# A forward chain dealt anew, one hand order over most of the kernel, and a backward sweep that starts ahead of its chain

## The chip, the core and the metric

The kernel runs on one core of a Trainium2 chip. The core has a matrix engine (PE, whose weight loads are shown apart as PEld), a vector engine (DVE), a scalar engine (ACT), a general engine (POOL) and a synchronising engine (SP); each runs its own instructions in order, and waits on semaphores for the others. Transfers are issued from SP, or from POOL, and run on 16 DMA engines. PE writes into PSUM, a small memory of banks; everything else lies in SBUF or in device memory. The metric is the device time of one execution in microseconds. Lower is better.

## What is computed

A gate mixes two networks over the same 2048 tokens of width 576, and the kernel returns the output and the gradients of every input.

```python
def _A_ref(x, wq, wk, wv, wo):          # 32 heads of 18, one shared key and value
    scores = einsum('bhqd,bkd->bhqk', q, k) * Dh ** (-0.5)
    o = einsum('bhqk,bkd->bhqd', softmax(scores), v)
    return o.transpose(...).reshape(B, S, H * Dh) @ wo
def _B_ref(x, mem0, Wq, Wk, Wv, Wo, seg_len):   # 32 heads of 128, segments of 32 tokens
    for s in range(n_seg):
        h = concatenate([mem, xs], axis=1)       # 8 memory tokens and 32 of the segment
        q, k, v = (einsum('btd,dhe->bhte', h, W) for W in (Wq, Wk, Wv))
        p = softmax(where(mask, einsum('bhqe,bhke->bhqk', q, k) * scale, -1e9))
        o = einsum('bhte,hed->btd', einsum('bhqk,bhke->bhqe', p, v), Wo)
        mem = o[:, :M, :]                        # goes into the next segment
g = sigmoid((x * gate_w).sum(-1)); out = g * _A_ref(...) + (1 - g) * _B_ref(...)
```

Network B is a recurrence: the memory rows of a segment must be done before the next begins, forward, and after it, backward. Network A has no such order.

## The kernel before

The kernel runs in stages: a setup with A's projections, the projections of grad_out and x through B's weights, a **forward weave**, a bulk stage for the tokens of B (`b_bulk`), a **backward weave**, the token gradients (`b_post`), the weight gradients (`b_dw`), and A's end. Each stage has its own pools of SBUF and PSUM tiles; a tile of a new pool that lies where an old one lay waits for the old one's last user.

`weave` takes two generators. The *chain* does the recurrence of B on the 8 memory tokens of each of 64 segments, cut by `yield` into 16 pieces a segment; the *sweep* does A's attention, 1024 steps of one key block against one pair of heads. A weave issues one piece and then one step, in that order on every engine; `lead` is how many steps go first (2 forward, none backward).

*A forward sweep step* (`a_pass1`): PE computes S of the next step (`a_S`, one buffer) and dP of this one, ACT the exponential `a_E` of S, DVE the product `a_W` of dP and `a_E`, in two halves, and PE adds `a_W` and `a_E` times the keys and values to `a_acc`. After 16 steps a block of 512 queries is done; `a_post` turns it, in three parts at the steps 2, 3 and 5 of the next 16: PE transposes the sums (`a_acs` into `a_tk`) and the block's QD, ACT copies the latter to `a_qt`, and POOL normalises and scales, with three stores from SP.

*A forward chain segment* (`b_chain_fwd`): projections of q, k and v for 32 rows, in units `proj(w, j, kts, name)` of up to five quartets of matmuls each (one quartet an element of kts), into the PSUM tiles `c_x` or `c_pj` (one buffer each); transposes by selection (`mem_T`); scores into c_x, their exponential c_E, the denominators `den` into a new c_x, the reciprocal `c_rd` on DVE, `c_pn`, its expansion `c_PB` on POOL; the output `po` and c_oT; and `heads(lo, hi)`, four matmuls a head through Wo, in two pieces of 16 heads. `rows_out`, `rows_copy`, `head_out` and `mT_out` store results; `load_k` and `load_v` fetch c_kx and c_vx for the next segment; `stash` and `stash_end` transpose a weight through SP into st_WT.

*Around the weaves.* At the end of `a_pass1` four small transposes go through `a_dlT`, which shares its one buffer with `a_qt`, to dl_dram. `b_bulk` builds two masks and zeroes four tiles on POOL, and loads its chunks (x_q, x_dO, x_k and others) from SP into the same pool as its results. Before the backward weave `load_WoT` loads WoT; the chain's first segment loads its inputs and then the weights WT (14.2 MB in six transfers, `load_WT`), and the backward sweep (`a_pass2`) loads a chunk of QD and SD for every four steps.

The two weaves, `b_bulk`, `b_post` and the two projection stages are issued in the order written; what lies between them (load_Wo, make_WoT, load_WoT, the last part of the setup) is ordered by a scheduler.

## Time and profile before

Three runs took 6164.37, 6149.91 and 6148.34 us, the median 6149.91 us. The profiled execution took 6158.5 us, its span is 6156.7 us.

| stage | from, to (us of the span) | length | PE busy | DMA share |
|---|---|---|---|---|
| setup, A's projections | 0, 184 | 184 | 138.59 | 0.43 |
| load of Wo, WoT | 184, 215 | 31 | 15.13 | 0.85 |
| projection of grad_out | 215, 361 | 146 | 137.54 | 0.61 |
| projections of x | 361, 500 | 139 | 130.92 | 0.41 |
| forward weave | 500, 2313 | 1813 | 1731.88 | 0.60 |
| bulk stage | 2348, 3060 | 712 | 654.01 | 0.93 |
| backward weave | 3098, 4765 | 1667 | 1515.68 | 0.42 |
| token gradients | 4775, 5345 | 570 | 548.55 | 0.96 |
| weight gradients | 5378, 6055 | 677 | 669.74 | 0.71 |
| end of A | 6055, 6157 | 102 | 87.49 | 0.27 |

Over the whole span PE is busy 92%, DVE 61%, ACT 56%, POOL 32%. A row of the timeline gives start and duration of one instruction or a run of like ones, and in brackets how long its engine had been idle before it and what ended that. A busy PE isn't always PE at its peak: the granted clock of a stretch says how fast it ran.

### The profile page before, as it was taken

The page shows a single profiled execution, that of the slowest core. Times are in us where ns is not written, and L with a number is a line of the kernel's source. Part 1 is how long each engine was busy: PE and PEld are TensorE (multiplying, and loading weights), DVE is VectorE, ACT ScalarE, POOL GpSimd, SP SyncE. Part 2 cuts the span into 40 slices and gives each one's busy share as a digit, 9 for nine tenths or more (in the row PEclk, how much of TensorE's full clock was granted, in tenths as well). Part 3 has the DMA queues.
Part 4 walks back from the last instruction along what each step waited for, and adds up shares of the span by engine and source line. Part 5 has one row for each costly group of instructions (what it writes and reads, how often), then busy time and mean ns, then how long its engine had stood idle before and what let it go on. Part 6 is the DMA issues. An engine that isn't in the chain of part 4 may idle for free.

```text
span 6156.7 us, 211396 instructions
## 1 busy us (share of the span) xinstructions
PE 5649.8 (92%) x90123; PEld 3274.8 (53%) x90334; DVE 3760.5 (61%) x7124; ACT 3435.7 (56%) x4916; POOL 1957.9 (32%) x3483
## 2 busy tenths in 40 slices
PE   7898999999999996999869999999998999899999
PEld 4543444444444445777735555555555777675444
DVE  4336778777778884666568888888888111111112
ACT  3325777777777774665557777777777222111101
POOL 3002333333333344444423333333333111112213
PEclk7999999999999998999989999999999999999999
DMA  4645666666665548999864443434343999896663
GB/s 151 224 154 115 126 125 130 122 128 126 125 127 115 108 86 231 253 255 254 248 196 109 108 108 109 109 108 108 109 108 98 242 248 246 228 278 200 216 186 112
DMA packets 1369174, 990.03 MB, mean 161 GB/s; under 512 B 931805, under 2 KB 1186790, under 8 KB 1357510
## 3 DMA queue, kind: packets, MB, share of 16 engines
q1 hardware_dynamic: 1286870, 782.63, 51.6%
q0 software_dynamic: 81360, 193.86, 9.8%
q8 instruction: 708, 11.60, 0.8%
q14 instruction: 236, 1.93, 0.1%
HBM read 550.31 MB, written 385.03 MB: 152 GB/s over the span
## 4 chain that ended last, share of the span: by engine, by line
PE 40%; ACT 11%; DMA 6%; issue 3%; SPq 1%; POOL 1%; DVE 0%; POOLq 0%; DVEq 0%; ACTq 0%
ACT b_E L1577 11%; PE w_acc L73 10%; PE b_S L73 6%; PE y_pdx L73 4%; PE r_pj L73 4%; DMA dsx_dram<-x_dS 3%; PE r_x L73 2%; PE x_tr L78 2%; PE b_acc L73 2%; PE y_pk L73 1%; PE x_po L73 1%; PE x_b L73 1%; PE x_m L73 1%; PE b_dP L73 1%; PE f_big L73 1%
## 5 line engine op out<-in xcount | busy, mean ns | idle before, releaser
L1469 DVE TENSOR_TENSOR a_W<-a_dP,a_E 128x512 bf16<-128x512 f32 x2048 | 1316.1, 685 | 357.5 <-issue 133.4
L1598 DVE TENSOR_TENSOR b_dS<-b_dP,b_E 128x512 bf16<-128x512 f32 x2048 | 1313.6, 683 | 240.8 <-issue 121.9
L1577 ACT ACTIVATE b_E<-b_S 128x1024 bf16<-128x1024 f32 x1024 | 1047.8, 1023 | 447.1 <-PE b_dP L73 322.7
L1439 ACT ACTIVATE a_E<-a_S 128x1024 bf16<-128x1024 f32 x1024 | 1049.4, 1025 | 358.0 <-PE a_dP L73 233.9
L73 PE MATMUL b_S<-b_KV,b_QD 32*128 32x512 bf16 x2048 | 400.1, 381 | 158.8 <-ACT b_E L1577 101.6
L73 PE MATMUL r_pj<-WT,r_dT 128*32 128x288 bf16 x12288 | 491.8, 287 | 0.6 <-DMA WT<-st_WT 0.6
L73 PE MATMUL w_acc<-w_d,w_h 128*128 128x512 bf16 (+1 forms) x2352 | 471.0, 379 | 2.5
L73 PE MATMUL a_S<-a_QD,l_KV 32*128 32x512 bf16 x2048 | 401.3, 384 | 39.7 <-ACT a_E L1439 17.9
L73 PE MATMUL b_acc<-b_dS,b_SD 128*32 128x512 bf16 x2048 | 418.7, 390 | 0.9 <-DVE b_dS L1598 0.7
L73 PE MATMUL a_acc<-a_W,l_WK 128*32 128x512 bf16 x4096 | 413.1, 391 | 1.8 <-issue 1.2
L73 PE MATMUL a_acc<-a_E,l_VK 128*32 128x512 bf16 x4096 | 403.8, 383 | 1.8 <-issue 1.8
L73 PE MATMUL b_acc<-b_E,b_SD 128*32 128x512 bf16 x2048 | 403.2, 390 | 0.0
L73 PE MATMUL a_dP<-a_QD,l_KV 32*128 32x512 bf16 x2048 | 399.6, 387 | 0.5 <-issue 0.5
L73 PE MATMUL b_dP<-b_KV,b_QD 32*128 32x512 bf16 x2048 | 398.3, 385 | 0.0
L1063 DVE COPY y_T<-y_pt 128x512 bf16<-128x512 bf16 x256 | 97.1, 420 | 460.2 <-PE y_pt L78 460.2
L73 PEld LDWEIGHTS <-r_dT 128*32 128x32 bf16 x12288 | 332.5, 97 | 79.3 <-issue 1.3
L73 PEld LDWEIGHTS <-w_h 128*128 128x128 bf16 (+1 forms) x2688 | 229.9, 100 | 258.3 <-issue 6.6
L73 PEld LDWEIGHTS <-b_QD 32*128 32x128 bf16 x4096 | 165.0, 91 | 348.5 <-issue 284.3
L73 PEld LDWEIGHTS <-hm 128*32 128x32 bf16 x7680 | 196.8, 96 | 226.0 <-issue 49.9
L73 PEld LDWEIGHTS <-l_KV 32*128 32x128 bf16 x4096 | 129.2, 91 | 300.6 <-issue 264.1
L1049 ACT CAST y_tdk<-y_pk 128x512 bf16<-128x512 f32 x128 | 75.0, 586 | 376.7 <-PE y_pk L73 211.7
L73 PE MATMUL y_pdx<-WT,y_T 128*128 128x288 bf16 x2048 | 273.0, 287 | 0.0
(422 smaller groups left out, 11232.7 us busy)
## 6 DMA issues: line engine op xcount, KB each, us to landing
b_QD<-qd_dram SPq DMA_DIRECT2D x256, 128.0 KB
b_SD<-sd_dram SPq DMA_DIRECT2D x256, 128.0 KB
dOx_dram<-p_tok SPq DMA_DIRECT2D x16, 1024.0 KB
c_vx<-vx_dram SPq DMA_DIRECT2D x256, 64.0 KB
krow_dram<-c_k POOLq DMA_DIRECT2D x64, 256.0 KB
qrow_dram<-c_q POOLq DMA_DIRECT2D x64, 256.0 KB
vrow_dram<-c_v POOLq DMA_DIRECT2D x64, 256.0 KB
x_q<-qx_dram SPq DMA_DIRECT2D x32, 512.0 KB
```

The lines of the kernel that those rows point to most:

```text
L73: return self.nc.tensor.matmul(out, lhsT, rhs, start=start, stop=stop, tile_position=tp, skip_group_check=True)
L78: return self.nc.tensor.transpose(out, in_, self.identB[b:b + nrows, b:b + nrows], tile_position=tp)
L1049: nc.scalar.copy(d[w][:, r, :], pk[:])
L1063: nc.vector.tensor_copy(T_[t][w][:], pt[:])
L1439: nc.scalar.activation(E_[n][:], S.pop(n)[:], ACT.Exp, scale=SCALEA)
L1469: nc.vector.tensor_tensor(out=W_[n][:, i, :], in0=dP[i][:], in1=E_[n][:, i, :], op=ALU.mult)
L1577: nc.scalar.activation(E_[n][:], S.pop(n)[:], ACT.Exp, scale=SCALEA)
L1598: nc.vector.tensor_tensor(out=D_[n][:, i, :], in0=dP[i][:], in1=E_[n][:, i, :], op=ALU.mult)
```

## The change

- *Forward chain.* Still 16 pieces a segment, filled differently: the k and q projections start with single quartets and swap c_x and c_pj; the mask is added with four 64-column matmuls; scores, den and the low half of v's second unit (`vlo`, 256 columns) share one c_x tile `px`; the high half goes to c_pj and is copied by DVE; the heads are in three pieces of 11, 10 and 11; `load_v` stands before `head_out`.
- *a_post.* QD is no longer transposed on PE and copied on ACT; SP fetches it with a transposing transfer from qd_dram. The f32 transposes are split, one at step 1 and three at step 2. The last block's three stores go through POOL's queue.
- *One hand order* from load_Wo to b_post, with no scheduler between the stages.
- *Bulk stage.* The masks are built in `setup_B_consts`, the four tiles are zeroed on DVE, and the loads have a pool `xl`.
- *Backward weave.* The sweep leads by 12 steps, and does 10 more after the chain's pieces 5 and 8; WoT is loaded inside `b_chain_bwd`; WT comes in halves of its columns (rows of 576 bytes) instead of halves of its heads.

```diff
@@ setup_B_consts
+        mb = pool.tile([P, 64], BF16, name="mbias")
+        nc.gpsimd.memset(mb[:], NEGB)
...
+        mx = pool.tile([P, 4, P], BF16, name="maskX")
+        mxm = pool.tile([P, 4, 32], BF16, name="maskM")
+        nc.gpsimd.memset(mx[:], 0.0)
+        nc.gpsimd.memset(mxm[:], NEGB)
+        for j in range(4):
+            nc.gpsimd.affine_select(out=mx[:, j, :], in_=mx[:, j, :], compare_op=ALU.is_ge, fill=NEGB,
+                                    base=0, pattern=[[-1, P]], channel_multiplier=1)
...
+        self.maskX, self.maskM = mx, mxm
@@ weave, proj_cols
-    def weave(self, chain, sweep, per_piece, lead=0):
-        with self.tc.manual_schedule():
-            for _ in range(lead):
-                next(sweep)
-            for _ in chain:
-                for _ in range(per_piece):
-                    next(sweep, None)
-            for _ in sweep:
-                pass
+    def weave(self, chain, sweep, lead, extra=()):
+        for _ in range(lead):
+            next(sweep)
+        extra = dict(extra)
+        for i, _ in enumerate(chain):
+            for _ in range(1 + extra.get(i, 0)):
+                next(sweep, None)
+        for _ in sweep:
+            pass
...
+                        start=(kt == 0), stop=(kt == NKT - 1), tp=(0, 32 * c))
+
+    def proj_cols(self, out, st, Wt, lo, n, kts):
+        for kt in kts:
+            for c in range(4):
+                self.mm(out[32 * c:32 * c + 32, :], lhsT=st[:, kt, :], rhs=Wt[:, kt, c * 1024 + lo:c * 1024 + lo + n],
                         start=(kt == 0), stop=(kt == NKT - 1), tp=(0, 32 * c))
 
@@ b_chain_fwd
             yield
-            proj("k", 0, (0, 1, 2), "c_x")
-            yield
-            proj("k", 0, (3, 4), "c_x")
-            proj("k", 1, (0,), "c_pj")
-            yield
-            proj("k", 1, (1, 2, 3), "c_pj")
-            yield
-            proj("k", 1, (4,), "c_pj")
-            proj("q", 0, (0, 1), "c_x")
-            yield
-            proj("q", 0, (2, 3, 4), "c_x")
-            yield
+            proj("k", 0, (0,), "c_pj")
+            yield
+            proj("k", 0, (1, 2, 3), "c_pj")
+            yield
+            proj("k", 0, (4,), "c_pj")
+            proj("k", 1, (0, 1, 2), "c_x")
+            yield
+            proj("k", 1, (3, 4), "c_x")
+            proj("q", 0, (0,), "c_pj")
+            yield
+            mT_out("k", self.mem_T(t2["k"], psum, "c_x", 1))
             rows_out("k")
-            proj("q", 1, (0, 1, 2), "c_pj")
+            proj("q", 0, (1, 2), "c_pj")
+            yield
+            proj("q", 0, (3, 4), "c_pj")
+            proj("q", 1, (0,), "c_x")
             if s < 48:
                 wt = stash(2 * s)
             yield
-            proj("q", 1, (3, 4), "c_pj")
-            mT_out("k", self.mem_T(t2["k"], psum, "c_x", 1))
+            proj("q", 1, (1, 2, 3, 4), "c_x")
+            rows_copy("k")
             yield
             src = self.mem_T(t2["q"], psum, "c_x", 1)
             qT = sp.tile([P, 8, 4, 8], BF16, name="c_qT", bufs=1)
...
-            rows_copy("k")
-            ps = psum.tile([P, P], F32, name="c_x", bufs=1)
-            self.mm(ps[:], lhsT=self.identB[:], rhs=self.mbias[:], start=True, stop=False)
+            px = psum.tile([P, 512], F32, name="c_x", bufs=1)
+            ps, den = px[:, 0:P], px[:, P:192]
+            for c in range(4):
+                self.mm(px[32 * c:32 * c + 32, 64:128], lhsT=self.identB[:, 32 * c:32 * c + 32],
+                        rhs=self.mbias[:], start=True, stop=False, tp=(0, 32 * c))
...
+            nc.scalar.activation(Et[:].rearrange("p a b -> p (a b)"), ps, ACT.Exp, scale=SCALEB)
+            proj("v", 0, (2, 3), "c_pj")
+            yield
+            proj("v", 0, (4,), "c_pj")
+            self.mm(den, lhsT=self.blockones[:], rhs=Et[:, 0, :], start=True, stop=False)
+            self.mm(den, lhsT=self.blockones[:], rhs=Et[:, 1, :], start=False, stop=True)
             rd = sp.tile([P, 64], F32, name="c_rd", bufs=1)
-            nc.vector.reciprocal(rd[:], den[:])
-            if not last:
-                kx = load_k(s + 1)
-            yield
-            proj("v", 1, (0, 1, 2), "c_x")
+            nc.vector.reciprocal(rd[:], den)
             pn = sp.tile([P, 2, 64], BF16, name="c_pn", bufs=1)
             nc.vector.tensor_tensor(out=pn[:], in0=Et[:], in1=rd[:].unsqueeze(1).to_broadcast([P, 2, 64]), op=ALU.mult)
             PB = sp.tile([P, 16, 4, 8], BF16, name="c_PB", bufs=1)
             self.expand(PB[:], pn[:].rearrange("p a (u q) -> p (a u) q", q=8), 16)
             nc.gpsimd.dma_start(self.pm_dram[s], pn[:].rearrange("p a b -> p (a b)"))
-            yield
+            if not last:
+                kx = load_k(s + 1)
+            vlo = px[:, 256:512]
+            self.proj_cols(vlo, h_, self.W["v"], 512, 256, (0, 1, 2))
+            yield
+            self.proj_cols(vlo, h_, self.W["v"], 512, 256, (3, 4))
+            nc.scalar.copy(t2["v"][:, 4:6, :].rearrange("p u e -> p (u e)"), vlo)
+            pv = psum.tile([P, 512], F32, name="c_pj", bufs=1)
+            self.proj_cols(pv[:, 0:256], h_, self.W["v"], 768, 256, range(NKT))
+            nc.vector.tensor_copy(t2["v"][:, 6:8, :].rearrange("p u e -> p (u e)"), pv[:, 0:256])
             rows_copy("q")
-            proj("v", 1, (3, 4), "c_x")
-            yield
+            yield
+            mT_out("v", self.mem_T(t2["v"], psum, "c_x", 1))
             po = psum.tile([P, 8, 32], F32, name="c_pj", bufs=1)
             for u in range(8):
                 self.mm(po[:, u, :], lhsT=vx[:, u, :], rhs=PB[:, u].rearrange("p c q -> p (c q)"), start=True, stop=False)
...
-            mT_out("v", self.mem_T(t2["v"], psum, "c_x", 1))
...
-            head_out()
...
-                heads(0, 16)
+                heads(0, 11)
+            yield
+            head_out()
+            if not last:
+                heads(11, 21)
             yield
             rows_copy("v")
             if not last:
-                heads(16, 32)
+                heads(21, 32)
                 hs = sp.tile([P, P], BF16, name="c_hs", bufs=1)
                 nc.vector.tensor_copy(hs[:], ph[:, 0:P])
@@ b_bulk
 
-    def b_bulk(self, wp, sp, psum):
+    def b_bulk(self, wp, lp, sp, psum):
         nc = self.nc
...
-            nc.gpsimd.memset(t[:], 0.0)
+        for t in mB["v"] + mB["k"]:
+            nc.vector.memset(t[:], 0.0)
         mT = {}
         C = {}
...
+                            mT[tt][x] = lp.tile([P, 4, HB, 8], BF16, name=f"x_{x}mT", bufs=2)
@@ load_WT, b_chain_bwd
     def load_WT(self):
-        for wi in (2, 0, 1):
-            for g in range(2):
-                self.nc.sync.dma_start(self.WT[wi][:, 16 * g:16 * g + 16, :], self.st_WT[wi][:, 16 * g:16 * g + 16, :])
+        for hf in range(2):
+            c = slice(288 * hf, 288 * hf + 288)
+            for wi in (2, 0, 1):
+                self.nc.sync.dma_start(self.WT[wi][:, :, c], self.st_WT[wi][:, :, c])
 
     def b_chain_bwd(self, keep, sp, psum):
         nc = self.nc
         NSEG = self.NSEG
         dm = [keep.tile([P, NKT, 32], BF16, name=f"dm{i}") for i in range(2)]
+        self.load_WoT(keep)
         mrow = {w: keep.tile([P, 8, n * E], BF16, name=f"r_{w}") for w, n in (("q", 1), ("k", 1), ("dx", 2))}
         pads = {w: keep.tile([P, n, 8, 32], BF16, name=f"r_{w}pad") for w, n in (("p", 1), ("ds", 1), ("x", 2))}
         for t in dm + list(mrow.values()) + list(pads.values()):
@@ a_pass1
                     bb = n // 16 - 1
-                    post = self.a_post(bb // 4, bb % 4, acs, QD.pop(bb), sp, xps, dl_all)
+                    QD.pop(bb)
+                    post = self.a_post(bb // 4, bb % 4, acs, sp, xps, dl_all)
             if n < NP_ and n % 16:
                 acc_mm(acc, n, E_, self.VK, False, False)
-            if post is not None and n % 16 in (2, 3, 5):
+            if post is not None and n % 16 in (1, 2, 5):
                 if next(post, "end") == "end":
                     post = None
             yield
...
             nc.scalar.copy(dlT[:], ptr[:].rearrange("p a b -> p (a b)"))
             nc.gpsimd.dma_start(self.dl_dram[:, t4 * 512:(t4 + 1) * 512], dlT[:])
@@ a_post
-        nc = self.nc
-        pt = psum.tile([P, 4, P], F32, name="c_pj", bufs=1)
+    def a_post(self, p, qb, acs, sp, psum, dl_all):
+        nc = self.nc
+        dq_ = nc.gpsimd if (p, qb) == (NPR - 1, self.T // 512 - 1) else nc.sync
+        qt = sp.tile([P, 4, 4, 32], BF16, name="a_qt", bufs=1)
+        nc.sync.dma_start_transpose(qt[:].rearrange("p a b c -> p a (b c)"), self.qd_dram[p][:, qb * 512:(qb + 1) * 512])
+        pt = psum.tile([P, 4, P], F32, name="c_x", bufs=1)
         for j in range(4):
             nc.tensor.transpose(pt[:, j, :], acs[:, j * P:(j + 1) * P], self.identF[:])
+            if j == 0:
+                yield
         tk = sp.tile([P, 4, 2, 64], F32, name="a_tk", bufs=1)
         tkf = tk[:].rearrange("p a b c -> p (a b c)")
         ptf = pt[:].rearrange("p a b -> p (a b)")
         nc.scalar.copy(tkf, ptf)
-        yield
-        pd = psum.tile([P, 4, P], BF16, name="c_pj", bufs=1)
-        for j in range(4):
-            self.tr(pd[:, j, :], QD[:, j * P:(j + 1) * P], P)
-        qt = sp.tile([P, 4, 4, 32], BF16, name="a_qt", bufs=1)
-        nc.scalar.copy(qt[:].rearrange("p a b c -> p (a b c)"), pd[:].rearrange("p a b -> p (a b)"))
         yield
         rl = sp.tile([P, 4, 2, 2], F32, name="a_rl", bufs=2)
         nc.vector.reciprocal(rl[:, :, 1, :], tk[:, :, :, 18])
...
-        nc.sync.dma_start(otd(self.otok_dram), ot[:].rearrange("p a b c -> p a (b c)"))
+        dq_.dma_start(otd(self.otok_dram), ot[:].rearrange("p a b c -> p a (b c)"))
@@ build_full
+        with ExitStack() as man:
+            man.enter_context(tc.manual_schedule())
+                k.load_Wo(bwo)
...
-                    k.weave(k.b_chain_fwd(a2k, cfs, cfp), k.a_pass1(a2k, a2s, a2p, cfp), 1, 2)
+                        k.weave(k.b_chain_fwd(a2k, cfs, cfp), k.a_pass1(a2k, a2s, a2p, cfp), 2)
+            with SB("xw") as xw, SB("xl") as xl, SB("xs") as xs, PS("xp") as xp:
+                k.b_bulk(xw, xl, xs, xp)
-                k.load_WoT(rk)
-                    k.weave(k.b_chain_bwd(rk, rs, rp), k.a_pass2(a3k, a3s, a3p), 1)
+                    k.weave(k.b_chain_bwd(rk, rs, rp), k.a_pass2(a3k, a3s, a3p), 12, ((5, 10), (8, 10)))
```

## The prediction

> **What bounds the kernel now.** I read first the windows, to see which stages leave PE idle; then the groups and the waits of the two weaves; then the timeline, step by step. In the windows the columns are length, busy time (and instructions) of PE, PEld, DVE, ACT and POOL, granted clock, DMA share, GB/s.
>
> ```profile
> 500.00:2313.00 1813.00, 1731.88 (x35522) 769.70 (x35523) 1439.85 (x2622) 1389.70 (x1792) 694.72 (x1438) 0.99 0.60 119
> 2313.00:2348.00 35.00, 2.34 (x16) 1.58 (x15) 0.00 (x0) 2.31 (x4) 15.56 (x25) 0.50 0.46 132
> ...
> 3060.00:3098.00 38.00, 8.46 (x90) 4.71 (x87) 4.66 (x8) 3.29 (x7) 7.72 (x13) 0.61 0.83 257
> ...
> 3098.00:3112.00 14.00, 11.27 (x230) 5.12 (x228) 9.36 (x18) 9.77 (x13) 3.78 (x6) 0.83 1.01 427
> 3112.00:3133.00 21.00, 0.39 (x16) 0.28 (x12) 0.50 (x1) 0.55 (x2) 1.20 (x3) 0.60 1.06 412
> ```
>
> The forward weave (1813 us) is PE-bound on average; three holes stand out: 35 us before the bulk stage, some 30 us before the backward weave, and 21 us inside it in which only the DMA engines work, at 412 GB/s.
>
> Inside the forward weave one segment is 16 sweep steps, each with one chain piece behind it. A step's floor is S, exp, S again, because a_S has one buffer: the a_S starts 1409.53 and 1411.08 below are 1.55 us apart.
>
> ```profile
> L1469 DVE TENSOR_TENSOR a_W<-a_dP,a_E 128x512 bf16<-128x512 f32 x2048 | 1316.1, 685 | 357.5 <-issue 133.4
> L1439 ACT ACTIVATE a_E<-a_S 128x1024 bf16<-128x1024 f32 x1024 | 1049.4, 1025 | 358.0 <-PE a_dP L73 233.9
> ...
> L1512 ACT COPY a_qt<-c_pj 128x512 bf16<-128x512 bf16 x64 | 37.1, 580 | 0.7 <-PE c_pj L78 0.6
> ```
>
> The timeline around one softmax (start, duration; PE, then DVE, then PE's heads piece):
>
> ```profile
> 1407.84 0.39 PE L73 MATMUL a_S<-a_QD,l_KV 32*128 32x512 bf16 x2
> 1409.37 0.23 PE L73 MATMUL c_x<-c_E,blockones 128*128 128x64 bf16 x2
> 1409.53 0.39 PE L73 MATMUL a_S<-a_QD,l_KV 32*128 32x512 bf16 x2
> 1410.30 0.82 PE L73 MATMUL c_x<-Wv,hm 128*32 128x512 bf16 x12
> 1411.08 0.39 PE L73 MATMUL a_S<-a_QD,l_KV 32*128 32x512 bf16 x2
> ...
> 1408.36 1.29 DVE L1469 TENSOR_TENSOR a_W<-a_dP,a_E 128x512 bf16<-128x512 f32 x2 [0.33 <-ACT c_E L401]
> 1409.63 0.56 DVE L408 RECIPROCAL c_rd<-c_x 128x64 f32<-128x64 f32 x1
> ...
> 1415.83 0.91 PE L73 MATMUL c_pj<-WoN,c_oT 128*8 128x144 bf16 x42 [0.32 <-issue]
> ```
>
> The reader is to see that the sweep's own PE work takes 0.77 us (1409.53 to 1410.30), that the reciprocal c_rd waits on DVE for the step's two a_W and ends 2.35 us after that step's S (1407.84 to 1410.19), and that c_x is written again only at 1410.30.
>
> **Forward re-deal.** From each a_E to the next, averaged over the 64 segments, the 16 steps sum to 28.21 us: 24.80 of floor (16 x 1.55) and 3.41 over it. Of these the two heads steps are 0.97 (2.07 and 2.00), the two with a_post's transposes 1.67 (2.39 each), the rest 0.77.
> After: three heads pieces of 40 to 44 matmuls, 0.77 + 44 x 0.0174 (two such lines, 64 matmuls, fill 1.11) = 1.54, under the floor; but the idle on issue (0.32 above, 0.48 in the next piece) goes with the number of instructions, so I keep 0.70. The QD transposes (0.33 of PE) and the 0.22 wait for a_qt (0.58 on ACT) go; the f32 transposes (0.15 each) come 1 and 3. With 0.24 + 0.07 for a projection quartet, memT 0.3, scores 0.6, the other pieces stand over the floor by: n=2 0.07, n=4 0.25, n=6 0.11, n=8 0.27, n=9 0.15, n=10 0.55, n=12 0.12, three more 0.08. Sum 1.60.
> The piece of n=11 is the new wait. It puts den, c_rd's source, and the low columns of v into one tile px, so the first vlo matmul must wait for c_rd, in the same piece; before, a whole step lay between them. PE is at S + 0.77 + 0.31 (v0 quartet) + 0.16 (den) = S + 1.24; c_rd ends at S + 2.35, the matmul starts near 2.40 and the next S stands behind twelve 256-column matmuls (0.42): step 2.82, 1.27 over the floor, of which 1.17 is the wait. Everything behind it on PE, the next S first, waits too. Sum 1.60 + 1.27 + 0.70 = 3.57 against 3.41: +0.16 x 64 = **+10 us**. Bounds: without the wait 10 - 75 = -65; with nothing of the issue stalls hidden and the 0.42 us DVE copy of vhi (nearest row c_qT, 0.42) in the way of a_W, +60.
> The Trainium skill, "PSUM — Partial Sum Buffer", Terms, says that two engines must not touch one bank in the same quadrant at once; by that rule the wait would be there even with separate tiles in that bank, and it speaks against putting den and vlo together. Before, den's c_x is likewise rewritten (1410.30) only after c_rd has read it (1410.19).
> SP gets 64 more DMA transposes; the like c_wt ones take 1.19 us of SP. SP's waits in the weave include 217.6 us for POOL c_oh, and head_out now stands behind the c_vx loads, so I let the two cancel and price a late SP in a rival. POOL's a_qt multiply then waits for a landing instead of ACT; POOL is busy 695 of 1813 us, which covers it.
>
> **The two holes between stages.**
>
> ```profile
> 2331.78 0.58 ACT L1493 COPY a_dlT<-c_x 64x512 bf16<-64x512 bf16 x1 [20.02 <-DMA sd_dram<-a_qt]
> ...
> 2343.66 0.33 SPq L577 DMA_DIRECT2D x_q<-qx_dram  x1
> ...
> 3072.73 10.81 SPq L839 DMA_TRANSPOSE r_vxT<-vx_dram  x1
> ...
> 3093.57 4.84 SPq L820 DMA_DIRECT2D WT<-st_WT  x6
> 3098.49 0.40 SPq L1556 DMA_DIRECT2D b_QD<-qd_dram  x1
> ...
> 3133.05 0.61 PE L73 MATMUL b_S<-b_KV,b_QD 32*128 32x512 bf16 x2 [20.66 <-DMA b_QD<-qd_dram]
> q1 hardware_dynamic: 1286870, 782.63, 51.6%
> ```
>
> *Before the bulk stage.* POOL builds masks and memsets from 2305.4 to 2320.9 between a_post's last operations, a_dlT waits 20 us for a store of the tile it shares, and x_q is issued only at 2343.66, PE starting at 2347.25. After, the loads have their own pool and stand right behind the last chain DMAs; a_dlT has two buffers of another tag; the last stores go to POOL's queue (three, 0.55 each). The POOL chain from a_rl to a_qt needs some 6 us without the memsets, four dl stores 0.55 each and about 2 to land, and the first x_qT copy waits for these: about 2323 instead of 2347, **-24 us** (-12 if the four stores stay serial over 12 us; -32 if the loads alone decide, the stage being DMA-bound).
>
> *Before and in the backward weave.* The sweep's loads now come first on SP behind the store at 3067.06 (3.5 us), so the first b_S starts near 3075.5 instead of 3097.5. But SP is in order. QD and SD of the fourth and fifth chunk wait for steps 4 and 9 to free buffers, so WoT is issued near 3092.5; then r_vmT 0.7, r_vxT 10.8, and the run from r_pT to r_q 7.5 (3083.59 to 3091.13): WT at about 3113 instead of 3093.6. The sixth chunk's QD is issued behind all six WT loads. In the rows above a QD issued just behind WT (3098.49) was there only at 3133.05: the queue is first in, first out, so it took 35 us. The lead of 12 and six interleaved steps use 18 of the 20 steps loaded, the ten extra ones stop after two, and PE with its hand order stands still until that QD lands.
> How long WT takes is unknown: its rows shrink from 18,432 to 576 B, 24,576 packets. Lower bound 14.2 MB at 412 GB/s, 34 us. Upper: the queue's mean packet is 608 B and took 39.5 ns (51.6% of 16 x 6156.7 us over 1,286,870), so 24,576 x 39.5 / 16 = 61 us. I take 47, between: QD lands at 3161 (3147 to 3175).
> By the Trainium skill, "DMA: Bandwidth & Descriptors", Specifications, rows of 512 B and more still run at line rate; that would be the 34 us, and a sum 13 us lower.
> From 3161: 18 lone steps x 1.55 = 28, then 986 pairs x 1.606 ((4765 - 3133) / 1016), then 32 chain pieces without a sweep, two segments. One costs at least its own PE work, 11.5 us (1515.7 / 64 - 16 x 0.76), at most its 26 in the weave; I take 17.5 for the evacuations between: 35. End 3161 + 28 + 1583 + 35 = 4807 against 4765: **+42 us** (+16 with 3147 and 23; +73 with 3175 and 52).
>
> **Start.** POOL builds the masks in the setup, ahead of the a_wo loads (9.48) and xtail that PE waits for (12.11, 33.51): the same operations took 2305.4 to 2311.1, 5.7 us; **+5** (0 to 8). The four p_x loads stand on SP behind the st_WoT stores (204.69, 10.43 long), so the first projection starts near 218 instead of 214.59: **+3** (0 to 5).
>
> **Sum.** +10 - 24 + 42 + 5 + 3 = +36. The profiled execution took 6158.5 us (span 6156.7), 8.6 over the median of the runs shown, 6149.91; I put the sum on the median: 6186.
>
> **Rivals.**
> *A, faster: the reciprocal isn't in vlo's way.* If DVE is ahead at that place, so that c_rd runs as soon as den is there (S + 1.24), 1.17 x 64 = 75 us go: 6111. For it: a_W's row has 357 us idle, and the 0.33 ahead of the a_W at 1408.36 need not recur. Against: DVE works in order, both a_W are issued first and need that step's dP. It decides from a wait under 0.6 us.
> *B: the early sweep does what it is for.* The QD of chunk six lands without WT's backlog; then no 21 us hole, S 22 us earlier, 35 of tail and 4 of WoT waiting: -5 instead of +42: 6139. Against it: the 20.66 row.
> *C, slower still: SP falls behind.* 64 transposes of 1.19 and a POOL that waits for their landing push PB and the k and v loads late by 1 us a segment: +64, 6250. For it: SP already waits 201.8 us on st_WT. Against: 0.60 DMA share, and SP's issue time is short of the 28 us.
>
> **How the numbers follow.** Main case 0.52, own range 6150 to 6222 (the backward bounds and half the forward ones), nearly all slower: 0.46 slower, 0.05 same, 0.01 faster. A 0.17, all faster. B 0.18: 0.09 faster, 0.07 same, 0.02 slower. C 0.13 slower. About 0.3% (18 us) is what a measurement can tell from no change. Faster 0.27, same 0.12, slower 0.61. The range runs from A to just short of C: 6108 to 6245.
>
> **What would show it.** Right: PE c_x<-Wv 32x256 idle on DVE c_rd, 1.1 to 1.2 us, 64 times; PE idle some 40 us on DMA b_QD after the twentieth b_S; two bare segments at the end of the backward weave; x_tr near 2323; no L1512 copy. Wrong: that wait absent, or b_QD landing before WT.

## The result and the profile after

The changed kernel took 6243.35 us (median of four runs, 6236.93 to 6248.59) against 6157.14 for the kernel before on the same chip: a ratio of 1.0138, with an interval of 1.0115 to 1.0161. It is 86 us slower where 36 were forecast. Its profiled execution has a span of 6234.9 us, 78.2 over that of before. Told by the first and last PE instruction of each stage's tiles:

| from, to | before | after | difference | forecast |
|---|---|---|---|---|
| start to the first p_pb | 214.6 | 222.0 | +7.4 | +8 |
| first p_pb to the first a_S | 286.1 | 289.8 | +3.7 | 0 |
| forward weave, first to last a_S | 1804.1 | 1856.5 | **+52.4** | +10 |
| last a_S to the first x_tr | 42.5 | 22.1 | -20.4 | -24 |
| bulk stage | 718.9 | 717.0 | -1.9 | 0 |
| last x_po to the first b_S | 31.3 | 8.3 | -23.0 | } |
| first to last b_S | 1663.5 | 1693.1 | +29.6 | } +42 |
| last b_S to token gradients | 12.1 | 49.4 | +37.3 | } |
| token gradients | 604.8 | 594.6 | -10.2 | 0 |
| weight gradients, end of A | 778.7 | 782.1 | +3.4 | 0 |

The three backward rows make +43.9. The -10.2 of the token gradients is no gain to count on: in the experiments below, kernels with the same code there took 594 to 608 us.

The windows of the changed kernel, in the columns of the prediction's:

```profile
515.00:2368.00 1853.00, 1708.18 (x36689) 781.48 (x36689) 1465.46 (x2680) 1337.94 (x1723) 690.98 (x1402) 0.99 0.63 121
2368.00:2392.00 24.00, 7.41 (x70) 4.01 (x67) 7.18 (x11) 5.03 (x9) 10.37 (x22) 0.63 0.74 187
...
3160.00:3195.00 35.00, 0.00 (x0) 0.00 (x0) 0.00 (x0) 0.00 (x0) 0.00 (x0) 0.50 1.12 323
4809.00:4847.00 38.00, 31.08 (x760) 21.83 (x756) 7.30 (x20) 8.29 (x19) 17.33 (x30) 0.87 0.23 58
```

Between the first and the last a_S PE is busy 17 us less than before (1709.7 against 1726.9) in 52 us more time, so it isn't the amount of work that grew. The last two rows are the stop behind WT, in which no engine does anything, and the bare tail, in which PE has 760 matmuls in 38 us.

The backward part of the timeline has the forecast's queue in its order:

```profile
3131.23 0.33 SPq L1576 DMA_DIRECT2D b_QD<-qd_dram  x1
...
3133.87 1.47 SPq L555 DMA_DIRECT2D WoT<-st_WoT  x3
...
3147.86 37.30 SPq L840 DMA_DIRECT2D WT<-st_WT  x6
...
3192.87 0.38 SPq L1576 DMA_DIRECT2D b_QD<-qd_dram  x1
...
3196.34 0.61 PE L75 MATMUL b_S<-b_KV,b_QD 32*128 32x512 bf16 x2 [40.15 <-DMA b_QD<-qd_dram]
```

WoT is held until 3133.87 by the buffers that the lone steps must free, the first WT is issued at 3147.86, and the b_S that needs the next QD starts at 3196.34 after 40.15 us of idle.

The waits of the forward weave of the changed kernel (waiting engine and line, what it waited for, us in total, times, longest):

```profile
POOL a_qt L1559 <- DMA a_qt<-qd_dram: 226.0, 51, 10.4
...
ACT a_E L1459 <- issue: 102.1, 72, 4.6
...
PE c_x L75 <- DVE c_rd L432: 65.4, 64, 2.2
...
PE c_pj L75 <- issue: 26.5, 23, 4.1
...
PE c_pj L75 <- POOL c_PB L236: 8.5, 9, 1.9
```

The wait on c_rd is there 64 times, 1.02 us each. So the forecast's new wait came nearly as it was priced (1.17), and the 42 us that were not forecast are elsewhere. To find them, take each of the 16 steps of a segment (from one a_E to the next) by its median over the 64 segments, and what its mean is over that, its excess: the median shows the deal of the work, the excess what happens in some segments only.

| us a segment | before | after | difference x 64 |
|---|---|---|---|
| medians of 16 steps | 27.28 | 27.41 | +8 |
| excess, first six steps (the heads in three of them, a_post) | 0.88 | 0.97 | +6 |
| excess, last four steps (scores, softmax, po) | 0.02 | 0.62 | **+38** |
| other | 0.03 | 0.03 | 0 |

The median of the step with the c_rd wait is 2.77 us (2.82 forecast), and the medians in all give +8 (with the wait). The rest is irregular: 38 of 52 us are in the last four steps, which had no irregular loss before; PE's idle on issue there (it waits for nothing that the profile shows), in gaps over 0.4 us, went from nothing to 12 us. By what PE does, the 40 us of excess that these steps have are 13 of idle on issue, 8.5 of waiting for c_PB and 16 of PE being busy longer than in the median; over all steps the 104 us of excess (59 before) are 41 of idle on issue (28) and 34 of longer busy time (17). Four rows of the timeline of one segment (start, duration, engine; in brackets the idle time before) show an irregular stop in a heads piece, five more how SP comes to be late:

```profile
1283.38 0.39 PE L75 MATMUL a_S<-a_QD,l_KV 32*128 32x512 bf16 x2
...
1288.81 0.52 PE L75 MATMUL c_pj<-WoN,c_oT 128*8 128x144 bf16 x9 [4.15 <-issue]
...
1289.27 0.60 PE L75 MATMUL a_S<-a_QD,l_KV 32*128 32x512 bf16 x2
...
1289.96 1.02 ACT L1459 ACTIVATE a_E<-a_S 128x1024 bf16<-128x1024 f32 x1 [4.61 <-issue]
...
1298.32 1.22 SPq L1523 DMA_TRANSPOSE a_qt<-qd_dram  x1
...
1304.76 1.05 POOL L1559 TENSOR_TENSOR a_qt<-a_qt,a_rl 128x512 bf16<-128x512 bf16 x1 [1.20 <-DMA a_qt<-qd_dram]
...
1305.83 0.33 SPq L1562 DMA_DIRECT2D sd_dram<-a_qt  x1
...
1306.26 1.20 SPq L314 DMA_TRANSPOSE c_wt<-in_B_Wk_dram  x1
...
1307.31 0.40 PE L75 MATMUL c_x<-c_qT,c_kx 128*32 128x8 bf16 x32
```

At 1288.81 PE resumes in the midst of a heads piece, 35 of whose 44 matmuls ran before, after 4.15 us in which no wait had held it. (ACT's row ends in issue too, but its exponential starts 0.09 us after the end of the a_S that it reads, so it waited for PE.) Behind the stop an a_S takes 0.60 us, ahead of it 0.39: the granted clock is 0.50 from 1288.6 on, for 6.8 us. That is part of the longer busy time. Past the weave's first steps the clock stands at 0.50 eight times for 3.4 or 6.8 us, 34 us in all (before three times, 14 us), each time after PE had been idle for some 1.5 us or more of the 6.8 ahead. At 1298.32 SP issues the new transposing transfer a_qt; POOL multiplies its result, SP must store that (1305.83), and only then comes the next transposing transfer, c_wt, beside the scores piece (1307.31). SP is in order, so each transfer runs where SP has come to, not where the program has it: in the first 51 of the 64 blocks SP issues a_qt three to eight steps after PE has made the transposes beside which it is written, in the last 13 none to two.

The trace has a control in itself: weights are moved (c_wt, st_WT) in the segments 0 to 47 alone. In the segments 1 to 48 the excess is 1.83 us a segment, in 50 to 63 it is 0.45 (before: 1.00 and 0.11), and 33 of PE's 35 stops over 0.4 us lie before segment 50.

### The profile page after: what moved, and what is told of

Its sections match the earlier page's. It is cut to its first block, busy times and chain, and to the rows that moved or that the text cites. A ratio compares the mean times of both kernels' runs of the same rounds, so it can differ in the third digit from the quotient of the medians.

```text
span 6234.9 us, 214080 instructions
## 1 busy us (share of the span) xinstructions
PE 5645.8 (91%) x91339; PEld 3294.1 (53%) x91550; DVE 3794.9 (61%) x7192; ACT 3389.5 (54%) x4852; POOL 1955.4 (31%) x3481
## 4 chain that ended last, share of the span: by engine, by line
PE 34%; ACT 11%; issue 9%; DMA 5%; SPq 2%; POOL 2%; DVE 0%; POOLq 0%; DVEq 0%; ACTq 0%
ACT b_E L1597 10%; PE w_acc L75 10%; PE b_S L75 6%; PE r_pj L75 4%; PE r_x L75 3%; DMA dsx_dram<-x_dS 3%; PE x_tr L80 2%; PE b_acc L75 2%; PE x_po L75 1%; PE x_b L75 1%; PE x_m L75 1%; PE f_big L75 1%; PE b_dP L75 1%; PE x_S L75 1%; SPq L840 1%
## 5 line engine op out<-in xcount | busy, mean ns | idle before, releaser
L75 PEld LDWEIGHTS <-hm 128*32 128x32 bf16 x8960 | 226.6, 97 | 238.1 <-issue 79.6
```

Of the source, the lines that this page charges most:

```text
L75: return self.nc.tensor.matmul(out, lhsT, rhs, start=start, stop=stop, tile_position=tp, skip_group_check=True)
```

## The experiments

The runs are in five sets, each on a chip of its own, and the irregular stops differ by chip: the changed kernel itself had a ratio of 1.0225 on another. So kernels are compared with those of the same set and by ratio to the kernel before. The forward weave of the changed kernel runs unchanged in e3, e7 and e9, which are the controls of sets 1, 2 and 3. Sets 4 and 5 have none, and of before there is one trace, not one a chip. The table has for each run the forward weave by segment (its mean, the medians, the excess at the heads, first six steps, and at the softmax, last four); PE's idle on issue in gaps over 0.4 us at the same two places, us in the whole weave; and the backward weave from the last x_po to the token gradients.

| run | median us | ratio (interval) | mean | medians | excess | issue | backward |
|---|---|---|---|---|---|---|---|
| before |  | 1 | 28.21 | 27.28 | 0.88, 0.02 | 24, 0 | 1707 |
| after | 6243.35 | 1.0138 (1.0115 to 1.0161) | 29.03 | 27.41 | 0.97, 0.62 | 27, 12 | 1751 |
| *set 1* | | | | | | | |
| e1_qt_plain | 6222.41 | 1.0114 (1.0099 to 1.0129) | 28.67 | 27.42 | 0.54, 0.68 | 9, 1 | 1752 |
| e2_den_last | 6232.95 | 1.0130 (1.0115 to 1.0146) | 28.94 | 26.79 | 0.95, 1.17 | 10, 29 | 1750 |
| e3_lead0 | 6204.18 | 1.0084 (1.0068 to 1.0099) | 28.90 | 27.42 | 0.65, 0.80 | 15, 14 | 1716 |
| e4_quiet | 6171.20 | 1.0030 (1.0017 to 1.0044) | 27.92 | 27.38 | 0.16, 0.35 | 1, 0 | 1750 |
| *set 2* | | | | | | | |
| e5_before_quiet | 6326.48 | 1.0214 (1.0199 to 1.0229) | 30.80 | 28.48 | 0.34, 1.93 | 4, 0 | 1706 |
| e6_quiet_den | 6257.79 | 1.0101 (1.0084 to 1.0118) | 29.12 | 26.62 | 0.59, 1.84 | 2, 17 | 1751 |
| e7_lead6_spread | 6303.11 | 1.0180 (1.0163 to 1.0197) | 30.36 | 27.92 | 0.99, 1.42 | 20, 31 | 1711 |
| e8_all | 6213.47 | 1.0031 (1.0019 to 1.0043) | 28.99 | 26.59 | 0.47, 1.84 | 1, 13 | 1716 |
| *set 3* | | | | | | | |
| e9_after_again | 6316.77 | 1.0225 (1.0200 to 1.0249) | 30.09 | 27.68 | 0.90, 1.44 | 15, 28 | 1752 |
| e10_wt_quiet | 6230.84 | 1.0090 (1.0072 to 1.0109) | 28.53 | 27.41 | 0.45, 0.62 | 6, 10 | 1747 |
| e11_qt_early | 6299.06 | 1.0201 (1.0178 to 1.0225) | 29.70 | 26.87 | 1.28, 1.46 | 45, 59 | 1752 |
| e12_best | 6230.41 | 1.0094 (1.0073 to 1.0115) | 29.53 | 26.86 | 1.22, 1.37 | 38, 51 | 1706 |
| *set 4* | | | | | | | |
| e13_before_wt_quiet | 6243.16 | 1.0101 (1.0073 to 1.0128) | 29.46 | 27.31 | 1.99, 0.11 | 28, 0 | 1708 |
| e14_old_deal | 6214.92 | 1.0048 (1.0032 to 1.0063) | 29.49 | 27.29 | 2.00, 0.11 | 21, 0 | 1703 |
| e15_qt_quiet | 6333.51 | 1.0248 (1.0218 to 1.0277) | 30.37 | 27.41 | 1.01, 1.87 | 41, 9 | 1750 |
| e16_all_quiet | 6263.90 | 1.0135 (1.0107 to 1.0163) | 30.09 | 26.62 | 1.57, 1.84 | 56, 8 | 1704 |
| *set 5* | | | | | | | |
| **e17_stages_only** | **6161.17** | **0.9963 (0.9949 to 0.9978)** | 28.66 | 27.48 | 1.02, 0.04 | 13, 0 | 1704 |
| e18_quiet_stages | 6206.56 | 1.0038 (1.0023 to 1.0053) | 29.07 | 27.42 | 0.17, 1.37 | 1, 0 | 1705 |

The theories that an expectation numbers are those of its own set.

### Which transfer makes the stops: e1 and e4

e1 fetches QD by a plain transfer instead of a transposing one, at the same place (so QD lies untransposed in a_qt, and what is stored from it is not the scaled QD):

```diff
-        nc.sync.dma_start_transpose(qt[:].rearrange(...), self.qd_dram[p][:, ...])
+        nc.sync.dma_start(qt[:].rearrange(...), self.qd_dram[p][:, ...])
```

> The changed kernel with one edit: a_post's transfer of QD is a plain one of the same 128 KB, without the transpose (so sd_dram holds untransposed rows and what is computed from it differs). The forward weave's steps were 29.03 us a segment against 28.21 before; their medians explain 0.13 of that, the rest is idle of PE on issue, 1.62 us a segment over the medians against 0.93. Theory 1, the 64 new transposes (512 packets of 256 B each) delay the fetch of instructions: the excess falls back to about 0.95, the run is 40 to 45 us faster than the changed kernel, near 6200. Theory 2, the excess comes from the new deal itself (where its own loads and its dense pieces now lie): it stays at 1.4 to 1.6, the run within 12 us of the changed kernel, near 6240.

e4 leaves a_qt as it is and moves the others: c_kx and both c_wt of a segment are written among the projections, in its first pieces:

```diff
             if s:
+                kx = load_k(s)
...
             proj("k", 0, (1, 2, 3), "c_pj")
+            if s < 48:
+                wt = stash(2 * s)
...
-            if not last:
-                kx = load_k(s + 1)
...
-                if s < 48:
-                    stash_end(*wt)
-                    wt = stash(2 * s + 1)
```

> The changed kernel with the forward chain's own transposing transfers (c_kx and the two c_wt of a segment) issued in the pieces 0 to 5, where PE has 40 to 56 instructions a step, instead of beside the scores and the heads, where it has 90 to 180; a_post's stay. Theory 1, PE idles on issue where such transfers run beside dense pieces: the excess over the medians falls from 1.62 to under 0.9 us a segment, the run is 40 to 60 us faster, near 6190. Theory 2, the idle goes with the density of instructions alone: the excess stays above 1.4, the run within 15 us of 6243.

Against the control on the same chip, e3 with 28.90 us a segment, e1 takes 0.23 a segment (15 us) and e4 0.98 (63 us), with the medians unmoved (27.42, 27.42, 27.38): all of it is excess, 1.48 in the control, 1.25 and 0.54. e4 stands below the weave of before (27.92 against 28.21, though on another chip). The waits of e4:

```profile
PE c_x L75 <- DVE c_rd L436: 63.7, 64, 1.1
...
POOL a_qt L1558 <- DMA a_qt<-qd_dram: 41.2, 15, 3.9
PE c_x L75 <- DMA c_kx<-kx_dram: 13.6, 10, 2.5
...
PE c_pj L75 <- issue: 1.1, 3, 0.7
```

PE's idle on issue is all but gone (29 us in gaps over 0.4 us in the control, 1 here), POOL's wait for a_qt is 41 us where the control had 271, and the c_rd wait is unmoved. What is left irregular is mainly a c_kx that now lands late in ten segments. So most of the excess hangs on where the chain's transposing transfers stand in SP's order, with the same deal of the work. By which way isn't separated: e4 lowers PE's idle on issue, POOL's wait and PE's longer busy time (35 us in the control, 12) at once, while e1, which takes 20 us of the idle on issue away, leaves POOL's wait long (319 us).

### Is the c_rd wait worth taking away: e2, e6

Both write three quartets of vlo ahead of den, so that c_rd has nothing to hold up; e6 also has e4's order, with c_kx in the last piece.

```diff
-            self.mm(den, lhsT=self.blockones[:], rhs=Et[:, 0, :], start=True, stop=False)
+            vlo = px[:, 256:512]
+            self.proj_cols(vlo, h_, self.W["v"], 512, 256, (0, 1, 2))
+            self.mm(den, lhsT=self.blockones[:], rhs=Et[:, 0, :], start=False, stop=False)
```

> The changed kernel, with the first three quartets of vlo issued ahead of den in the same piece, so that no matmul of that piece waits for c_rd (PE idled 65.4 us on it in 64 places). Theory 1, that wait is on the path that sets the step: the step falls from 2.77 to about 1.7 us, the run is 55 to 70 us faster than the changed kernel, near 6180. Theory 2, what is waited for there is waited for again a piece later (vlo's last quartets, c_PB or a_W): less than 25 us come back, near 6225.

> The changed kernel with the quiet transfers (c_kx now issued at the head of the last piece, since it came up to 2.5 us late from piece 0) and with vlo ahead of den. Theory 1, taking the c_rd wait away bought only 6 us because PE then ran into the fetch of instructions (excess 1.62 to 2.14) and into c_PB: with the fetch out of the way the median gain shows, 27.2 to 27.4 us a segment, 30 to 45 us under the quiet run, near 6135. Theory 2, c_PB and a_W are the next bound whatever the fetch does: within 12 us of the quiet run, 6160 to 6180.

In e2 the wait is gone, and its step has a median of 1.58 instead of 2.77. Yet the weave takes 28.94 us a segment where the control e3 takes 28.90. The waits of e2:

```profile
POOL a_qt L1559 <- DMA a_qt<-qd_dram: 336.2, 51, 9.2
...
PE c_pj L75 <- POOL c_PB L236: 23.5, 29, 2.0
...
PE c_x L75 <- issue: 9.3, 11, 2.0
```

POOL stands longer before a_qt (336 us, 271 in the control), its c_PB comes later (23.5 us of waiting, 14.3 in the control), and PE, which used to arrive 1 us later, now waits for it; the step two further on has a median of 2.10 instead of 1.56. In all the medians fall by 0.63 a segment (40 us), and the excess rises by 0.66 (42 us): the wait on c_rd had covered late work of POOL and late instructions. Against its control e7, e6 gains 1.24 a segment, all of it in the medians (27.92 to 26.62); its excess is as high (2.50 against 2.44). As e6 has e4's order too, its gain isn't that of e2's edit alone.

### The order on SP: e5, e9 to e11, e13 to e16, e18

e5 is the kernel before with e4's move, line for line; e13 has the lines for c_wt alone.

> The kernel before, with the same move of c_kx and the two c_wt transfers into the pieces 0 to 5. Theory 1, transposing transfers beside dense pieces cost PE fetch time whatever the deal: the excess over the medians falls from 0.93 to 0.2 to 0.4 us a segment, the run is 30 to 50 us faster than the kernel before, near 6110; then the new deal as such is worth nothing, 27.4 us of medians against 27.3. Theory 2, only the new deal suffers from them: the run is within 10 us of 6150.

> The kernel before with the two c_wt transfers of a segment moved into the pieces 2 to 5, c_kx at its place. Theory 1, transposing transfers beside the heads keep PE's instructions waiting in either deal: PE's excess falls from about 0.9 to 0.2 to 0.4 us a segment and the run is 25 to 45 us faster than the kernel before. Then the new deal had nothing of its own to give, 27.4 us of medians against 27.3. Theory 2, the old deal pays nothing for them (its stalls are the density of the two heads pieces): within 10 us of the kernel before.

Both are slower than before. In e5 the idle on issue falls to 4 us as in e4, but c_kx is late instead (144.8 us in 39 waits of up to 6.9); in e13 c_vx is:

```profile
PE c_pj L73 <- DMA c_vx<-vx_dram: 48.0, 26, 3.6
PE c_pj L73 <- issue: 23.5, 18, 2.7
```

e9 is the changed kernel; e10 is e4 without its two edits for load_k; e11 adds e2's edit and writes a_qt at the 14th step of its own block, beside the heads of the segment, instead of the first step of the next.

```diff
+                if kt == 13:
+                    b = n // 16
+                    qts[b] = sp.tile([P, 4, 4, 32], BF16, name="a_qt", bufs=1)
+                    nc.sync.dma_start_transpose(qts[b][:].rearrange(...), self.qd_dram[...])
```

> The changed kernel once more, beside the runs of this call: its stalls differ from chip to chip (in the run with lead 6 on another chip the untouched forward weave took 30.36 us a segment, not 29.03). Both theories expect medians of 27.4 us a segment and an excess of 1.6 to 3; it is the measure for the three others.

> The changed kernel with the two c_wt transfers of a segment moved into the pieces 2 to 5 and c_kx left at its place. Theory 1, PE's fetch of instructions is late where transposing transfers run beside the heads, so moving these two is enough: PE's idle on issue falls to a few us in all, the excess by at least 0.8 us a segment, the run 45 to 75 us under the changed kernel of this call. Theory 2, it was c_kx's transfer (it stood beside the scores): the excess falls by less than 0.3, the run is within 20 us.

> As the run before, and vlo ahead of den, and a_post's transposing transfer of QD issued at step 13 of its own block instead of step 1 of the next (POOL waited 226 us in all for it in the changed kernel, and with vlo first PE waited for c_PB behind it). Theory 1, the gain of taking the c_rd wait away was given back to c_PB, which is late because POOL waits for that transfer: now POOL waits under 60 us for a_qt, PE under 10 us for c_PB, 26.8 to 27.2 us a segment, 40 to 60 us under the run before. Theory 2, c_PB is late for another reason (c_pn, or the stores POOL issues): PE still waits over 25 us for it, the gain is under 25 us.

The move of c_wt alone takes 86 us from the changed kernel on that chip (6316.77 to 6230.84), half of the excess at the heads and more than half at the softmax. e11 gives nearly all of it back. Its waits:

```profile
POOL a_qt L1562 <- DMA a_qt<-qd_dram: 28.7, 16, 3.8
...
PE c_pj L75 <- issue: 62.8, 42, 5.5
...
PE c_x L75 <- issue: 20.0, 19, 4.0
```

POOL no longer waits for a_qt and c_PB is in time, so the chain of e2 is cut where it should be; but the idle on issue is six times that of e10 (104 us against 16), at the heads and the softmax alike. So a third transposing transfer among the pieces with the most matmuls seems to bring back what e10 had taken away: in the segments 50 to 63, where no weight is moved, the heads still have an excess of 1.28 us in e11 and 0.21 in e10. It isn't shown by itself, as e11 has two edits over e10; e2 alone, on another chip, had 39 us of idle on issue, and 0.63 us at those heads.

e15 is e10 with a_qt at the seventh step of its own block (`kt == 6` in e11's lines); e16 adds e2's edit and the stages of e17. e18 is e4 with those stages.

> The changed kernel with the quiet c_wt, and a_post's transposing transfer of QD issued at step 6 of its own block (at step 13 it raised PE's idle on issue, at step 1 it was late for POOL). Theory 1, what counts is only whether it runs beside a dense piece: the excess falls to 0.3 to 0.6 us a segment, 30 to 50 us under what the quiet c_wt alone gave (a ratio of 1.009 to the kernel before), a ratio of 1.001 to 1.004. Theory 2, SP blocks on the tile's one buffer and everything behind it is late: a ratio of 1.009 or more.

> As the run before, with vlo ahead of den, lead 6 and WT by halves of its heads, masks and p_x early. If the fetch of instructions was what took the c_rd gain back, the forward weave now takes 26.8 to 27.3 us a segment and the run is 60 to 100 us under the kernel before. If den's order itself brings the idle back, the excess is over 1 us a segment again and the run no better than the kernel before.

> The changed kernel with the transposing transfers of c_kx and c_wt in the pieces 0 to 5, as in the quiet run, and the same stages as the run before. If the quiet order's 27.9 us a segment holds on this chip: 35 to 50 us under the kernel before, a ratio of 0.992 to 0.994. If SP's order is too tight for c_kx, as it was in the kernel before with the same move, the ratio is 0.998 or more.

In e15 SP itself stops: a_qt has one buffer, so the transposing transfer waits for the store of the last block. In e18 the issue stalls are gone as in e4 (1.5 us), and c_kx takes their place. The queue's waits of e15 on SP, then PE's of e18:

```profile
SPq L1482 <- DMA sd_dram<-a_qt: 264.1, 63, 7.3
```

```profile
PE c_x L75 <- DMA c_kx<-kx_dram: 51.1, 28, 3.8
...
PE c_pj L75 <- issue: 1.5, 3, 0.7
```

e16 gains 0.28 a segment on e15 by e2's edit: 0.79 in the medians, of which 0.5 come back as excess. None of the orders tried brought either deal below the time of before: e5, e13, e15 and e18 each made another transfer late, and e11 brought PE's stops back.

### The backward weave: e3, e7, e8, e12, e14

e3 has no lead and no extra steps; e7 leads by six and issues one WT transfer a piece.

```diff
-                    k.weave(..., 12, ((5, 10), (8, 10)))
+                    k.weave(..., 0, ())
```

```diff
-                if s == NSEG - 1 and k == 1:
-                    self.load_WT()
+                if s == NSEG - 1:
+                    self.load_WT(k)
...
-                    k.weave(..., 12, ((5, 10), (8, 10)))
+                    k.weave(..., 6, ())
```

> The changed kernel with no lead and no extra steps in the backward weave, all else as changed (WT still in rows of 576 B). In the changed kernel the first b_S came 23 us earlier than before, PE then stood still 41 us for a QD queued behind WT, and two segments ran without a sweep for 37.7 us. Theory 1, the early start buys a longer stop and a bare tail: without it the stop is that of WT alone, some 25 to 35 us, the tail is gone, the run is 20 to 45 us faster than the changed kernel, near 6205. Theory 2, the small rows of WT are the whole loss and the lead a gain: the run is as slow as the changed one or slower, 6243 to 6265.

> The changed kernel with a lead of 6 and no extra steps, and the six WT transfers issued one by one in the first pieces instead of all at once, so that a QD has at most a part of WT ahead of it. Theory 1, the loss is the order in the queue (SP blocked on buffers, then QD behind all of WT) and the bare tail: the stop falls from 41 to under 15 us in all, the tail to about 7, the first b_S stays some 23 us early, the run is 50 to 75 us faster than the changed kernel, near 6180. Theory 2, WT's bytes must pass before the chain can go on, whatever the order: the stops still add to 30 us or more, the run is no faster than with lead 0, 6200 or more.

e3 takes 35 us off the backward weave (1716 against 1751): all of the bare tail, while the first b_S is 21 us later and the stop 8 us shorter. e7 has no long stop, yet six steps of 6 to 12 us in place of it, and ends at 1711. Before has 1707. The next three join parts: e8 is e6 with e7's backward weave, the masks built in the projection stage and the p_x loads ahead of the st_WoT stores; e12 is e11 with the same, and WT in halves of its heads (18,432-byte rows) instead of columns; e14 is e12 with the forward chain, a_pass1 and a_post of before, and c_wt moved as in e13. The lines of e12 for the start and for WT:

```diff
+                    for m in range(3):
+                        k.proj_load(items, m, pds)
                     with PS("wop") as wop:
                         k.make_WoT(bwt, wop)
...
+                        k.make_masks()
...
-    def load_WT(self):
...
+    def load_WT(self, i):
+        wi, g = (2, 0, 1)[i // 2], i % 2
+        self.nc.sync.dma_start(self.WT[wi][:, 16 * g:16 * g + 16, :], self.st_WT[wi][:, 16 * g:16 * g + 16, :])
```

> Quiet transfers, vlo ahead of den, lead 6 with WT spread, and two edits at the start: the masks are built by POOL in the projection stage where it is idle, and the first three p_x loads stand ahead of the st_WoT stores (PE waited 6.63 us for them). If the parts are independent the gains add up: about 105 in the forward weave, 60 in the backward, 7 at the start, near 6065, below the kernel before. If a part's cover is lost when another goes, the run is above 6100.

> All of it: quiet c_wt, vlo first, the early transfer of QD, masks built in the projection stage, p_x loaded ahead of the st_WoT stores, lead 6, and WT in six transfers by halves of its heads (rows of 18,432 B, as before the change), one a piece. If WT's small rows are the rest of the backward loss (45.6 us of stops with rows of 576 B however ordered, 24 before), the stops fall under 25 us; the run is 150 to 190 us under the changed kernel of this call and 50 to 90 under the kernel before. If not, the backward weave keeps over 40 us of stops and the run stays within 40 us of the kernel before.

> The forward chain, a_post and a_pass1 of the kernel before (with the quiet c_wt), and of the change the one hand order, the bulk stage's own pool and masks; the backward weave with lead 6 and WT by halves of its heads, one a piece; masks built in the projection stage and p_x ahead of the st_WoT stores. If the stages are independent: 25 to 45 us from the transfers, 20 from the gap ahead of the bulk stage, 0 to 5 from the rest, together 45 to 70 us under the kernel before. If the gap's gain depends on the new a_post, under 35.

The backward weave takes 1716, 1706 and 1703 us, so the long rows are worth some 5 to 12. A lead of six, a lead of none, one WT transfer a piece or six at once: within 13 us it is the same, and 4 us at best below before. The time of WT's 14.2 MB is paid in each, in one stop or in many: what the first 60 steps take over 1.6 us adds up to 36 to 50 us in these runs, 54 in the changed kernel and 26 before. The start is 8 us shorter with the two edits (213.7 in e8 against 222.0).

### The version that beats both: e17

The parts that stood each test are put on the forward weave of before, with its SP order untouched: the one hand order, the bulk pool, a_dlT's own buffers, the last stores on POOL, the masks in the projection stage, p_x early, a lead of six with WT one transfer a piece in halves of its heads. It is e14 without the move of c_wt.

> The kernel before with its forward chain, a_pass1 and SP order untouched (but a_dlT's tag and POOL's queue for the last block's stores), and around it the one hand order, the bulk stage's own pool, masks built in the projection stage, p_x ahead of the st_WoT stores, the backward weave with lead 6 and WT by halves of its heads, one a piece. If the stages' gains stand by themselves: 20 us from the gap ahead of the bulk stage and 0 to 5 from the backward weave, 18 to 28 us under the kernel before, a ratio of 0.995 to 0.997. If the forward weave is touched by them, over 0.998.

It takes 6161.17 us against 6183.43 on that chip, 0.9963 with an interval of 0.9949 to 0.9978: 22 us. Against the profile of before, the gap ahead of the bulk stage gives 21 (21.5 us against 42.5) and the backward weave 3. Its windows from the bulk stage's end:

```profile
3076.00:3084.00 8.00, 0.14 (x3) 0.00 (x0) 0.00 (x0) 0.59 (x1) 3.73 (x7) 0.60 0.67 203
3084.00:3130.00 46.00, 24.08 (x313) 8.32 (x314) 21.00 (x34) 17.71 (x21) 9.01 (x16) 0.65 1.01 356
```

PE is busy 24 of the 46 us in which the weights pass, at a DMA share of 1.01; before, it was busy 8.46 + 11.27 + 0.39 of 73 from 3060 to 3133.

## Why the prediction was right or wrong

*The failed step* is the one that says "the idle on issue (0.32 above, 0.48 in the next piece) goes with the number of instructions, so I keep 0.70". It made a constant, tied to the heads pieces, of what depends on when the transposing transfers run. For the three heads pieces themselves it was right: they stand over the floor by 0.67. But the sum has no other irregular loss. Of the 3.57 us a segment that it has over the floor, 2.87 are regular (1.60 and 1.27) and 0.70 irregular; measured are 4.23, of which 2.61 are in the medians, 17 us better in the whole weave, and 1.62 are excess, 59 us worse: 0.66 at the heads, 0.32 in the three steps behind them and 0.62 in the last four. These last four are what is new, with 0.02 before, and they have 38 of the 52 us by which the weave grew. e4 and e10 take more than half of the excess away without touching the deal. The same paragraph let two changes on SP cancel (217.6 us of waiting for c_oh gone, head_out behind c_vx). The wait for c_oh did go (4.1 us are left); but SP now waits 141 us for a_qt and its product before sd_dram, and 141 instead of 82 for krow_dram.

*The c_rd wait* was right in place and size: 64 times, 65.4 us in all where 75 was forecast, the step 2.77 us where 2.82 was. Rival A is out: c_rd is in vlo's way. What the forecast missed is that its price is hardly had back: without it nothing is gained in e2 and 0.28 a segment (18 us) in e16 against e15, as c_PB and PE's stops on issue are next. The bound of -65 for "without the wait" was therefore no bound to lean on.

*Rival C* named the right place, SP and POOL's wait for a landing (226 us on a_qt), and it was dismissed with the DMA share of 0.60, an average over the weave. It put the loss into late PB and late k and v loads; of these c_PB is there (8.5 us here, 21.5 on the chip of e9), and the larger parts of the last four steps' 40 us, PE's idle on issue (13) and its longer busy time (16), it did not have.

*The gap before the bulk stage*: -20.4 where -24 was forecast. The loads no longer decide it; a_dlT does. Its third transposition stands 12.37 us until the first dl_dram stores, which queue on POOL behind the last block's, have landed; the forecast's bound of -12 for serial stores had this mechanism.

*The backward weave*: +43.9 where +42 was forecast, and each part of it stood: first b_S 23.0 us earlier (22), stop at the twentieth step (41.3 us between two b_E; "some 40"), tail +37.3 (35). Rival B is out: QD is first in, first out behind WT. WT took 45.6 us from its first packet to its last, where 47 was taken (before, in rows of 18,432 bytes, 35.4).

By the Trainium skill, "DMA: Bandwidth & Descriptors", Specifications, rows of 512 bytes and more run at line rate. The runs don't bear this out: a packet of 576 bytes took 32 ns, which is 18 bytes a nanosecond, one of 18,432 bytes 690 ns (before), which is 26.7, and the windows have 323 GB/s against 412.

*The start*: +7.4 where +8 was forecast, split otherwise: xtail is 3.6 us later on PE (5 forecast for the masks), and PE then waits 6.6 us for p_x (3 forecast). The +3.7 in the projections was not forecast, and its cause is open.

## What to carry to other kernels

When one queue issues loads, stores and transposing transfers in order, a new transfer is priced by what it delays behind it and by what then runs beside the stages densest in instructions, not by its own time; look for where the queue really stands, not where the program writes the transfer. Before removing a wait, ask which late arrival it covers: the next one may be 1 us behind it, as c_PB was behind c_rd. And split a step's mean into its median and its excess: a deal changes the medians, a late queue the excess, and the two are cured differently.

## What was not expected of the hardware

*PE's stops on issue come where the DMA engines are busy, and look like waits for instructions.* In the three microseconds ahead of the 20 stops over 0.4 us at the heads pieces of the changed kernel the 16 DMA engines were 89% busy (54% with packets of 256 bytes, the size of the transposing transfers' packets); in the 163 such steps without a stop it was 77% (21%). Before, it was 90% (46%) and 67% (26%). At the last four steps of the changed kernel the engines were 89% busy ahead of the 13 stops and 59% in the steps without, but packets of 256 bytes had 15% in both, so there the stops aren't tied to the transposing transfers' own packets. Of the 51 stops over 0.7 us in e11, 37 end between 1 and 2 us after the last transfer of the instruction queues landed, where 18 of 100 moments taken at random do; of the 23 in the changed kernel 14 (the one of 4.15 us shown above isn't among them), of the 17 before 13. That the stops are waits for instructions is read from these packets and not shown by an experiment; that the order of the transfers brings them about is shown by e4 and e10, which move transfers alone, and that their kind matters by e1, which makes one of them plain (29 us of idle in gaps over 0.4 us in the control, 9 in e1).

*A stop can cost more than its length.* The excess is not idle time alone: a third of it in the changed kernel, and about half of it in e9, is PE being busy longer than in the median step (34 of 104 us, 75 of 154). In e9 the granted clock stood at 0.50 for 123 us of the weave, in the changed kernel's first trace for 55, before for 41, in e4 for 38. In the changed kernel 15 of the 34 us lie in steps that the lowered clock touches; what lengthens the others isn't known.

By the Trainium skill, "Runtime: NRT & Kernel Launch", Instruction fetch mechanics, the sequencer fetches ahead in blocks, and the cost of a block's end is mostly hidden. Here it is mostly hidden too (375 such transfers for all engines in the weave of the changed kernel, and 23 stops of PE over 0.7 us), but those 23 stops are 32 us.

*Chips differ in it.* The changed kernel's weave took 29.03 us a segment on one chip and 30.09 on another, the medians 27.41 and 27.68; three quarters of the difference are excess (1.62 and 2.40).

What stays open: why the c_kx and c_vx loads land in time in one order on one chip and not on another (e4 against e18); whether the new deal, whose medians are 26.6 to 26.9 without the c_rd wait against 27.3 before, can be worth its 0.4 to 0.7 us a segment with transfers on a second queue, which was not tried; and how the idle on issue splits between the number of matmuls in a piece and the load on the DMA engines.
